# A first feed-forward group without partial products, and three small moves in the order of GpSimd, ScalarE and VectorE work

## The chip, the cores and the metric

The kernel runs on one core of one Trainium2 chip. The metric is device time in microseconds from the first to the last instruction. Before the change it is 1409.2 us, the median of three runs (1407.0 to 1409.7). The profiled execution has a span of 1406.5 us, with a mean granted TensorE clock of 0.99.

## The reference, cut to what matters

Two blocks follow each other. The first is attention with a threshold, for 8 batches, 8 heads, 576 positions and a head width of 64; the second is a layer norm with a feed-forward block and a residual, on 512 features with 2048 hidden ones.

```python
scores = scale * np.matmul(q, k.transpose(0, 1, 3, 2))
thresh = np.max(scores, axis=-1, keepdims=True) - tau
scores = np.where(scores >= thresh, scores, -1000000000.0)
scores = scores - np.max(scores, axis=-1, keepdims=True)
attn = np.exp(scores)
attn = attn / (np.sum(attn, axis=-1, keepdims=True) + 1e-09)
return np.matmul(attn, v).astype(np.float32)
...
x = np.ascontiguousarray(attn_out.transpose(0, 2, 1, 3)).reshape(B, S, H * D)
...
xn = (x - mu) / np.sqrt(var + 1e-06) * g_ln
ch = np.maximum(xn @ w_ch1, 0.0) @ w_ch2
return (x + ch).astype(np.float32)
```

All of it is in float32.

## The kernel before, in words

**Two streams, interleaved.** Attention goes in 72 *slots*, nine for each of the 8 batches (`NS = B * SLOTS`, L65). Slots s = 0 to 3 and 5 to 8 of a batch treat a pair of heads and one half of its rows; slot 4 (`HP`) treats what is left over of all pairs. In a slot TensorE makes the scores (L394), VectorE takes their maxima (L408, `exponentials`), GpSimd makes the thresholds (L412), ScalarE the exponentials (L418), VectorE applies the threshold and sums the rows (L426), inverts the sums (L431), and GpSimd divides (L442, `weights`). VectorE then transposes the result by blocks into `et` (L508), which goes to memory and comes back as `em` for the product with the values in the next slot (L554). In the first batch this transposition is done by TensorE instead (L466, L482).

**The feed-forward groups.** When half of a batch's positions have their 512 features, they make a *group* of 288 tokens; there are 16 groups, two to a batch. `centre` (L606) subtracts the mean (L613) and leaves `xc`. Then `ffn_steps` (L1003) makes a generator that yields after each product on TensorE: `first_part` (w_ch1, ReLU, into `hidden`), then the second part (w_ch2), `second_plain` for group 0 and `second_quarters` for the others. Even groups start in slot 6 of their batch, odd ones in slot 2 of the next batch; groups 0 and 1 start in slots 6 and 10 of the whole.

**Tiles and quarters.** A *tile* is 128 hidden features for all 288 tokens: 8 matmuls (four `product` calls of two matmuls of 64 columns, L104), and a ReLU on ScalarE (L805). In all groups but group 0 six of the 16 tiles (`SETS`, 5 to 7 and 13 to 15) are replaced by seven *quarters*: a fast scheme of the Strassen-Winograd kind, which makes seven half-sized products in place of eight and needs sums and differences. The differences of the activations are three GpSimd operations (`less`, `add`, `less` at L842 to L844, into `t3`, `t2`, `t4`) and one on VectorE (`t1`, L848); the results are added on VectorE and GpSimd (L755) and clipped (L761). A quarter's bank is copied by ScalarE (L838). The differences of the weights are made once: `differences_1` (L703, eight operations on GpSimd and VectorE in a chain that goes back and forth between them) for w_ch1, `differences` (L719, 16 operations) for w_ch2. In the second part of the groups from 1 on, seven *segments* of 16 `product` calls each do the same for w_ch2 (L931 to L945), with differences of `hidden` on both engines (L929). Tiles, quarters and segments share two banks of PSUM (`ps_ff`, L79), so a product waits for the copy of the last but one.

**The norm.** `norm` (L773) is called after each tile and each quarter. It first has ScalarE square `xc` (L777) into a part of `hidden` that is free until later, and GpSimd add the four squares (L779, three additions). Some steps later it puts a product of these sums with a constant matrix on TensorE (`var`, L784), ScalarE turns it into a first root (L786 to L788), and three VectorE operations improve it (`root`, L674 to L678). `ended` counts finished tiles, `part` is the part of the slot in which the call falls.

**What sets the order.** The schedule is written out by hand: each engine works through its list in the order of these Python calls. A slot has four parts. `second_part` (L1037) is called once in each; it adds to `owed` the units that this part should do, from the units left in the group and from `ROOM` (L1013), shared out over the time to the next group's start, and steps the generator until it is used up:

```python
owed += (ends[g] - issued) * ROOM[i] / left if left > 0 else 8
got = 1 if i in (0, QUARTERS - 1) else 2
while queue and (owed >= 0.5 or got == 1 and i in (0, QUARTERS - 1)):
    got, cost = next(queue[0], (None, 0))
```

So parts 0 and 3 end only at the end of a tile, quarter or segment; parts 1 and 2 end anywhere. A tile costs 4 units, a quarter 3, a variance product 1, a segment 8. Between the parts lie the attention's own calls: in order, scores, maxima, two exponentials, part 0, two more exponentials, `turn` (the transposes of the next q and k, with a product on GpSimd, L342), part 1, `weights`, `drip`, part 2, `turn_blocks`, `drip`, the product with the values, part 3, `drip`.

**Lists of later calls.** `later` (L741) puts an operation into `rush` or `drops` with an engine, a cost and an age; `drip` (L622) issues those that are urgent and ripe, or for which there is room; `need` (L750) issues them at once where a product needs them. A `rush` entry for GpSimd at the head is also issued straight after part 0 (L1108).

Of the kernel before, what the change touches and what calls it, by code (L numbers as in the profile page):

```python
# [18 lines left out]
def kernel(  # L19
# [31 lines left out]
    nc = tc.nc  # L51
# [5 lines left out]
    NK = DM // 128  # L57
    ND = DF // 128
# [4 lines left out]
    SLOTS = 2 * HP + 1  # L63
    NG = 2 * B
# [3 lines left out]
    HT, HD, HM = TOK // 2, ND // 2, NK // 2  # L68
    SETS = [(5, 6, 7)]
# [547 lines left out]

    aside, stores, drops, rush = [], [], [], []  # L620

    def drip(room=None, everything=False):  # L622


        room = dict(room or {})
        for calls in (rush, drops):
            urgent = [i for i, d in enumerate(calls) if d[0] and d[1] <= now]
            n = urgent[-1] + 1 if urgent else 0
            while calls:
                _, ripe, eng, cost, go = calls[0]  # L630
                if n <= 0 and not everything:
                    if ripe >= now or room.get(eng, 0) < cost:
                        break
                    room[eng] -= cost
                calls.pop(0)
                n -= 1
                go()
# [112 lines left out]
    def need(calls, done, *what):  # L750
        while not done.issuperset(what):
            calls.pop(0)[-1]()

    def add(eng, out, a, b):
        eng.tensor_tensor(out=out, in0=a, in1=b, op=ALU.add)  # L755

    def less(eng, out, a, b):
        eng.tensor_tensor(out=out, in0=a, in1=b, op=ALU.subtract)
# [4 lines left out]
    def first_part(g, done):  # L763
# [1 line left out]

        xc = centred.pop(g)
        plain = g == 0
        low = ND - NK if plain else ND - 3 - NK
        sq = hidden[:, low : low + NK]
        rb, squared, ended = [], [], 0  # L770
        sums_of = differences() if g == 1 else iter(())

        def norm(must=False):  # L773

            if ended and not squared and (plain or part):
                squared.append(ended)
                nc.scalar.activation(sq, xc, func=AF.Square)  # L777
                for c in range(1, NK):
                    nc.gpsimd.tensor_tensor(out=sq[:, 0], in0=sq[:, 0], in1=sq[:, c], op=ALU.add)  # L779
            elif squared and not rb and (  # L780
                ended >= squared[0] + (7 if plain else 2) and part > (0 if plain else 1) or must
            ):
                var = ps_ff.tile([128, TOK], F32, tag="ff", name="var")
                product(var, lhsT=avg_sb, rhs=sq[:, 0], start=True, stop=True)  # L784
                rb.append(ffn.tile([128, TOK], F32, tag="rb", bufs=2, name="rb"))
                nc.scalar.activation(sq[:, 2], var, func=AF.Identity, bias=eps_sb)  # L786
                nc.scalar.activation(rb[0], sq[:, 2], func=AF.Ln)
                nc.scalar.activation(rb[0], rb[0], func=AF.Exp, scale=-0.5)  # L788
                later(
                    rush, done, ("root", 3, lambda _: root(rb[0], sq[:, 2], sq[:, 3]), nc.vector),  # L790
                    urgent=nc.vector, age=2 if part > 2 else 0,
                )
                return [(1, 1)]
            return []
# [44 lines left out]
            yield 2, 0.5  # L839

        def quarters():
            less(pool, t3, b22, b12)  # L842
            add(pool, t2, b11, t3)
            less(pool, t4, b21, t2)  # L844
            yield quarter(1, old(0, 0), b11, h11)
            yield quarter(2, old(0, 1), b21)
            yield quarter(7, s3, t3)
            later(rush, done, ("xt1", 1, less, dve, t1, b12, b11), urgent=dve)  # L848
            yield quarter(6, s2, t2, h12)
            later(  # L850
                rush, done, ("xu2", 1, add, dve, h12, h12, h11), ("xu3", 1, add, dve, parts[7], parts[7], h12),
                ("x11", 1, add, pool, h11, h11, parts[2]), ("r11", 1, positive, pool, h11),
            )
            need(rush, done, "xt1")
            yield quarter(4, old(1, 1), t4, h21)
            later(rush, done, ("x21", 1, add, dve, h21, h21, parts[7]), ("r21", 1, positive, dve, h21))
            need(rush, done, "x11")
            yield quarter(3, s4, b22)
            later(rush, done, ("x12", 1, add, dve, h12, h12, parts[3]))
            yield quarter(5, old(1, 0), t1, h22)  # L860
            later(
                rush, done, ("xu4", 1, add, dve, h12, h12, h22), ("r12", 1, positive, dve, h12),
                ("x22", 1, add, dve, h22, h22, parts[7]), ("r22", 1, positive, dve, h22),
                urgent=dve,
            )

        paired = set() if plain else {m + i for m in ms for i in (0, HD)}
        singles = [d for d in range(ND) if d not in paired]
        between = iter(()) if plain else quarters()
        for d in singles:  # L870
            while conversion.ended < 4 * (d // 4 + 1):
                yield 0, 0
            if d == low:
                yield from norm(True)
            if d == low + 2:
                need(rush, done, "root")
            yield from tile_of(d)
            for _ in range(2):
                next(sums_of, None)
            ended += 1  # L880
            yield from norm()
            if not plain and d > 1:
                yield from next(between, ())
                yield from norm()
        for more_of in between:
            yield from more_of
# [3 lines left out]

    def second_plain(g, rb, done):
        y = ffn.tile([128, NK, TOK], F32, tag="sq", bufs=1, name="y")
        sums_of = differences_1()
        for m in range(NK):
            p2 = ps_ff.tile([128, TOK], F32, tag="ff", name="p2")
            for d in range(ND):
                while conversion.ended <= conversion.n1 + 4 * m + d // 4:
                    yield 0, 0
                product(
                    p2, lhsT=w2_sb[:, m, d], rhs=hidden[:, d],  # L900
                    start=(d == 0), stop=(d == ND - 1),
                )
                if now >= QUARTERS * (SLOTS + 1) and d % 2:
                    next(sums_of, None)
                if d < ND - 1:
                    yield 2, 1
            aside.append(lambda m=m, p2=p2: add_to_x(g, m, y[:, m], p2, rb))
            yield 2, 1
        for _ in sums_of:
            pass  # L910

    def second_quarters(g, rb, done):


# [2 lines left out]
        s2, s3, s4 = more  # L917
        b11, b12 = hidden[:, :HD, early], hidden[:, :HD, late]
        b21, b22 = hidden[:, HD:, early], hidden[:, HD:, late]
        need(rush, done, "r21")  # L920
        while drops:
            drops.pop(0)[-1]()
        y = ffn.tile([128, NK, TOK], F32, tag="sq", bufs=1, name="y")
# [2 lines left out]
        def by_fours(eng, out, in0, in1, op):  # L926
            for d in range(0, HD, 4):
                at = (slice(None), slice(d, d + 4))
                eng.tensor_tensor(out=out[at], in0=in0[at], in1=in1[at], op=op)  # L929

        def segment(weights, rhs, out=None):  # L931
            bank = ps_ff.tile([128, HM, HT], F32, tag="ff", name="seg")
            for d in range(HD):
                for m in range(HM):
                    at, end = (d, m), (HD - 1, HM - 1)
                    product(
                        bank[:, m], lhsT=weights[:, m, d], rhs=rhs[:, d],
                        start=at == (0, 0), stop=at == end,
                    )
                    if at != end:  # L940
                        yield 2, 0.5
            if out is None:
                out = part_tile("part")[:, : HM * HT].rearrange("p (m t) -> p m t", t=HT)
            nc.scalar.copy(out, bank)
            return out  # L945
# [49 lines left out]
        while waiting_mean:  # L995
            mean_of(waiting_mean.pop(0))
        p3 = yield from last
        later(drops, done, ("12", 1, add, dve, y12, y12, p3), ("done12", 2, finish, pool, 0, 1, (0, 1)))
        yield 2, 0.5

# [2 lines left out]
    def ffn_steps(g):  # L1003
# [7 lines left out]


    ROOM = (0.6, 1.0, 1.25, 0.35)  # L1013
    STEPS = [1 + NK * ND * 2] + [
        1 + NK * ND * 2 - NK * ND // 8 - sum(NK * len(ms) for ms in SETS) // 4
    ] * (NG - 1)
    ends = [sum(STEPS[: i + 1]) for i in range(NG)]
    queue = []
    issued = part = now = 0
# [70 lines left out]
    for n in range(NS):  # L1090
# [74 lines left out]
        tick(6)  # L1165
        run_all(aside)
        drip({nc.vector: 2, nc.gpsimd: 0})
    while later_calls or queue or aside or stores or drops or rush:
        n += 1
        for i in range(QUARTERS):  # L1170
            run(n, i)
            second_part(n, i)
            run_all(aside)
            drip(everything=True)
            run_all(stores)
# [30 lines left out]
```

## Time and profile before

| what | value |
|---|---|
| median of three runs | 1409.2 us (1407.0 to 1409.7) |
| span of the profiled execution | 1406.5 us |
| VectorE busy | 1013.2 us, 72% |
| GpSimd busy | 725.2 us, 52% |
| ScalarE busy | 497.6 us, 35% |
| matmul of 288 columns in a tile, x2656 | 410 ns each as recorded, 351.9 us together |
| matmul of 144 columns in a quarter (`hidden`), x1440 | 289 ns each as recorded, 101.9 us together |
| GpSimd division L442, x252 | 840 ns each |
| GpSimd sum of squares L779, x48 | 878 ns each |
| VectorE maximum L408, x144 | 1350 ns each |

How to read it: the busy time of TensorE is the union of its records, which overlap, so 410 ns of one matmul isn't what it adds to the time; the distance between the starts of two tiles in the timeline is. The profile writes a tile's four products as 16 matmul records, and a quarter's six products as 24. PEld is the loading of weights, which overlaps the matmuls. "Waits" lists, for an engine and a line, how long it stood and what ended that. Busy shares are means over 72 slots; what a change in one slot is worth is read in the timeline of that slot.

### The profile page before, as it was taken

How to read it: one execution, taken by the hardware profiler on the slowest of the kernel's cores; microseconds unless marked ns; L12 is line 12 of the kernel's file. 1: busy time of each engine (PE TensorE's matmuls, PEld its weight loads, DVE VectorE, ACT ScalarE, POOL GpSimd, SP SyncE). 2: the span in 40 equal slices, each digit the busy share in tenths (PEclk: the TensorE clock that was granted, in tenths of full speed). 3: DMA queues.
4: the chain of work that ended last, by engine and by line, in shares of the span. 5: the costliest groups of instructions: out<-in, count | busy, mean ns of one | idle time of the engine just before them, and what ended most of it. 6: DMA issues, size and time to landing. Idle time of an engine off the chain costs nothing. (4 is left out here: it accounts for less than half of the span.)

```text
span 1406.5 us, 38066 instructions
## 1 busy us (share of the span) xinstructions
PE 1326.8 (94%) x16128; PEld 1043.7 (74%) x16128; DVE 1013.2 (72%) x1680; ACT 497.6 (35%) x985; POOL 725.2 (52%) x887
## 2 busy tenths in 40 slices
PE   4888979899999999999999999999999999999996
PEld 3665656677868777787968777786868777787876
DVE  5997867668777787877777787877877687777321
ACT  3877613133242423333232323333242333324120
POOL 2444445655455655555554654546554644656433
PEclk9999999999999999999999999999999999999998
DMA  9612345255855376455855376445755377444211
GB/s 230 172 62 84 92 113 150 100 184 144 202 157 165 123 199 154 144 178 140 216 153 170 108 197 186 144 158 152 199 161 166 124 190 182 145 145 144 77 18 18
DMA packets 316393, 205.64 MB, mean 146 GB/s; under 512 B 242368, under 2 KB 273856, under 8 KB 308160
## 3 DMA queue, kind: packets, MB, share of 16 engines
q1 hardware_dynamic: 311456, 202.62, 50.6%
q8 instruction: 127, 2.08, 0.6%
q10 hardware_dynamic: 4736, 0.59, 0.4%
q14 instruction: 42, 0.34, 0.1%
q0 software_dynamic: 32, 0.00, 0.0%
HBM read 119.41 MB, written 83.76 MB: 144 GB/s over the span
## 5 line engine op out<-in xcount | busy, mean ns | idle before, releaser
L104 PE MATMUL p<-xc,w 128*64 128x288 f32 x2656 | 351.9, 410 | 15.2 <-DVE xc L613 9.8
L408 DVE TENSOR_REDUCE neg<-sc 128x2 f32<-128x1152 f32 x144 | 188.5, 1350 | 230.6 <-PE sc L394 230.6
L104 PEld LDWEIGHTS p<-xc,w 128*64 128x64 f32 x2656 | 190.4, 138 | 131.2 <-DVE xc L613 15.3
L418 ACT ACTIVATE e<-sc,neg 128x576 f32<-128x576 f32 x288 | 197.3, 745 | 249.3 <-DVE neg L408 217.1
L442 POOL TENSOR_SCALAR e<-e,den 128x576 f32<-128x576 f32 x252 | 208.6, 840 | 115.2 <-DVE den L431 115.0
L104 PE MATMUL seg<-hidden,w 128*64 128x144 f32 x3840 | 247.3, 286 | 1.5 <-DVE hidden L929 1.5
L104 PEld LDWEIGHTS seg<-hidden,w 128*64 128x64 f32 x3840 | 234.9, 137 | 11.9 <-issue 7.6
L426 DVE SCALAR_TENSOR_TENSOR e<-sc,thr,e 128x576 f32<-128x576 f32 x288 | 222.4, 811 | 12.8 <-ACT e L418 12.1
L412 POOL TENSOR_SCALAR thr<-neg,low_sb 128x2 f32<-128x2 f32 x144 | 44.7, 310 | 256.2 <-DVE neg L408 251.9
L508 DVE STREAM_TRANSPOSE et<-e 128x1152 f32<-128x1152 f32 x112 | 150.8, 1363 | 24.7 <-POOL e L442 24.3
L394 PE MATMUL sc<-kT,qT 64*128 64x192 f32 (+3 forms) x1024 | 149.1, 424 | 19.6 <-DVE qT L354 10.0
L394 PEld LDWEIGHTS sc<-kT,qT 64*128 64x128 f32 x1024 | 93.7, 190 | 66.9 <-issue 16.9
L554 PE MATMUL sc<-em,v_in 128*64 128x256 f32 (+1 forms) x1408 | 132.4, 331 | 2.5 <-DMA em<-scr 1.9
L104 PE MATMUL seg<-hidden,stage 128*64 128x144 f32 x1920 | 123.4, 287 | 0.0
L104 PEld LDWEIGHTS seg<-hidden,stage 128*64 128x64 f32 x1920 | 117.6, 137 | 5.4 <-issue 4.0
L805 ACT ACTIVATE hidden<-p 128x288 f32<-128x288 f32 x166 | 68.6, 414 | 148.9 <-PE p L104 148.3
L104 PE MATMUL quarter<-hidden,w 128*64 128x144 f32 x1440 | 101.9, 289 | 14.7 <-ACT part L838 14.6
L104 PEld LDWEIGHTS quarter<-hidden,w 128*64 128x64 f32 x1440 | 88.8, 137 | 34.4 <-POOL thr L412 10.7
L554 PEld LDWEIGHTS sc<-em,v_in 128*64 128x64 f32 x1408 | 87.8, 138 | 31.4 <-DMA em<-scr 2.1
L929 POOL TENSOR_TENSOR hidden<-hidden 128x576 f32<-128x576 f32 x60 | 89.0, 1492 | 42.1 <-DVE hidden L761 26.0
L104 PEld LDWEIGHTS quarter<-xc,w 128*64 128x64 f32 x1080 | 67.5, 137 | 13.0 <-ACT hidden L805 4.3
L571 ACT COPY x<-sc 128x256 f32<-128x256 f32 x60 | 22.3, 372 | 154.3 <-PE sc L554 152.6
(175 smaller groups left out, 1639.2 us busy)
## 6 DMA issues: line engine op xcount, KB each, us to landing
scr<-et SPq DMA_DIRECT2D x63, 1152.0 KB, 4.4
em<-scr SPq DMA_DIRECT2D x63, 1024.0 KB, 5.9
out_dram<-x SPq DMA_DIRECT2D x256, 36.0 KB, 4.3
q_in<-in_q_dram SPq DMA_DIRECT2D x124, 72.0 KB, 3.5
k_in<-in_k_dram SPq DMA_DIRECT2D x120, 72.0 KB, 2.8
er<-scr SPq DMA_DIRECT2D x63, 128.0 KB, 5.9
v_in<-in_v_dram SPq DMA_DIRECT2D x28, 256.0 KB, 4.4
w<-in_moe_w_ch_dram SPq DMA_DIRECT2D x10, 512.0 KB, 5.5
```

What stands on the lines that cost most here:

```text
L104: nc.tensor.matmul(out[r], lhsT=lhsT[:, r], rhs=rhs, **flags)
L394: nc.tensor.matmul(sc[h][64 * i : 64 * i + 64 if s == HP else 128, at : at + n], lhsT=ql[r] if s == HP else qT[r, half, j * 128 : (j + 1) ...
L408: nc.vector.tensor_reduce(out=neg[:, i], in_=pairs[h], axis=AXL.X, op=ALU.max, negate=True,)
L412: nc.gpsimd.tensor_scalar(out=thr[:, i], in0=neg[:, i], scalar1=-1.0, scalar2=low_sb, op0=ALU.mult, op1=ALU.add,)
L418: nc.scalar.activation(es[:, i], blocks[i], func=AF.Exp, bias=neg[:, i : i + 1])
L426: nc.vector.scalar_tensor_tensor(out=es[:, i], in0=blocks[i], scalar=thr[:, i : i + 1], in1=es[:, i], op0=ALU.is_ge, op1=ALU.mult, accum_o ...
L442: nc.gpsimd.tensor_scalar(out=es[:, i], in0=es[:, i], scalar1=den[:, i : i + 1], scalar2=1.0, op0=ALU.mult, op1=ALU.mult,)
L508: nc.vector.transpose(et[:, :, 64 * h : 64 * h + 64].rearrange("p n (j c) -> p j n c", j=2), es[:, 2 * h : 2 * h + 2].rearrange("p j (n c) ...
L554: nc.tensor.matmul(dst[64 * h : 64 * h + 64], lhsT=vt[:, h, c, :] if c < J else vr[:, h, :], rhs=pick(em[:, :, c] if c < J else er, hp, h) ...
L571: nc.scalar.copy(x_of(g)[:, hp, :QH], pv)
L805: nc.scalar.activation(hidden[:, d], p1, func=AF.Relu)
L929: eng.tensor_tensor(out=out[at], in0=in0[at], in1=in1[at], op=op)
```

## The change

It has five parts.

1. **Group 1 plain in its first part.** `whole` (groups 0 and 1) takes the place of `plain` where the tiles are chosen: group 1 makes 16 tiles and no quarters. Its second part stays as it is. The differences of w_ch2, made during group 1's first part, go one to a tile instead of two. `STEPS` counts group 1's units accordingly (121 instead of 118).
2. **Differences of w_ch1 later.** As group 1 no longer needs them, they move from group 0's second part, in slot 10, to the segments of group 1's second part, two to a segment.
3. **Early differences in a third list.** The three GpSimd operations ahead of the quarters no longer stand in the generator's order; they go into a list `early_on`, which `drip` empties first, or `need` before quarter 7.
4. **Squares in the slot's second half.** For all groups but group 0 the squares wait for part 2 or 3 (`part > 1`), and quarters count in `ended`.
5. **Root later.** The root step always gets an age of two parts, where it had none if the variance product fell in parts 0 to 2.

Parts 3 to 5 are meant to let the attention's divisions and maxima go ahead of the norm's work.

```diff
-        for calls in (rush, drops):
+        for calls in (early_on, rush, drops):
...
         plain = g == 0
-        low = ND - NK if plain else ND - 3 - NK
+        whole = g < 2
+        low = ND - NK if whole else ND - 3 - NK
...
-            if ended and not squared and (plain or part):
+            if ended and not squared and (plain or part > 1 or must):
...
-                    urgent=nc.vector, age=2 if part > 2 else 0,
+                    urgent=nc.vector, age=2,
...
         def quarters():
-            less(pool, t3, b22, b12)
-            add(pool, t2, b11, t3)
-            less(pool, t4, b21, t2)
+            later(
+                early_on, done, ("xt3", 1, less, pool, t3, b22, b12),
+                ("xt2", 1, add, pool, t2, b11, t3), ("xt4", 1, less, pool, t4, b21, t2), urgent=pool,
+            )
             yield quarter(1, old(0, 0), b11, h11)
             yield quarter(2, old(0, 1), b21)
+            need(early_on, done, "xt4")
             yield quarter(7, s3, t3)
...
-        paired = set() if plain else {m + i for m in ms for i in (0, HD)}
+        paired = set() if whole else {m + i for m in ms for i in (0, HD)}
...
             if d == low:
                 yield from norm(True)
+                yield from norm(True)
...
             yield from tile_of(d)
-            for _ in range(2):
-                next(sums_of, None)
+            next(sums_of, None)
             ended += 1
             yield from norm()
-            if not plain and d > 1:
+            if not whole and d > 1:
                 yield from next(between, ())
+                ended += 1
                 yield from norm()
...
     def second_plain(g, rb, done):
-        sums_of = differences_1()
...
-                if now >= QUARTERS * (SLOTS + 1) and d % 2:
-                    next(sums_of, None)
...
     def second_quarters(g, rb, done):
...
+        sums_of = differences_1() if g == 1 else iter(())
...
+                if d % 4 == 3:
+                    next(sums_of, None)
...
-    STEPS = [1 + NK * ND * 2] + [
-        1 + NK * ND * 2 - NK * ND // 8 - sum(NK * len(ms) for ms in SETS) // 4
-    ] * (NG - 1)
+    STEPS = [
+        1 + NK * ND * 2 - (NK * ND // 8 if g else 0) - (NK * len(SETS[0]) // 4 if g > 1 else 0)
+        for g in range(NG)
+    ]
```

More of the change, by code (lines that the diff above doesn't have):

```diff
@@ L615, in centre @@
             )
-    aside, stores, drops, rush = [], [], [], []
+    aside, stores, drops, rush, early_on = [], [], [], [], []
     def drip(room=None, everything=False):
         room = dict(room or {})
-        for calls in (rush, drops):
+        for calls in (early_on, rush, drops):
             urgent = [i for i, d in enumerate(calls) if d[0] and d[1] <= now]
@@ L865, in quarters @@
             )
-        paired = set() if plain else {m + i for m in ms for i in (0, HD)}
+        paired = set() if whole else {m + i for m in ms for i in (0, HD)}
         singles = [d for d in range(ND) if d not in paired]
-        between = iter(()) if plain else quarters()
+        between = iter(()) if whole else quarters()
         for d in singles:
@@ L908, in second_plain @@
             yield 2, 1
-        for _ in sums_of:
-            pass
     def second_quarters(g, rb, done):
@@ L919, in second_quarters @@
         b21, b22 = hidden[:, HD:, early], hidden[:, HD:, late]
-        need(rush, done, "r21")
+        if g > 1:
+            need(rush, done, "r21")
         while drops:
@@ L997, in second_quarters @@
         p3 = yield from last
+        for _ in sums_of:
+            pass
         later(drops, done, ("12", 1, add, dve, y12, y12, p3), ("done12", 2, finish, pool, 0, 1, (0, 1)))
@@ L1167 @@
         drip({nc.vector: 2, nc.gpsimd: 0})
-    while later_calls or queue or aside or stores or drops or rush:
+    while later_calls or queue or aside or stores or drops or rush or early_on:
         n += 1
```

## The prediction

> **What bounds the kernel now.** I read the page's busy times first, then the waits of TensorE alone, then timelines of the stretches in which TensorE has gaps.
>
> ```profile
> PE 1326.8 (94%) x16128; PEld 1043.7 (74%) x16128; DVE 1013.2 (72%) x1680; ACT 497.6 (35%) x985; POOL 725.2 (52%) x887
> ```
>
> TensorE is busy for 1326.8 of 1406.5 us and runs its list in order, so what counts is what lengthens or fills its 80 us of idle time. TensorE's waits in total, times, longest:
>
> ```profile
> PE quarter L104 <- ACT part L838: 14.6, 13, 4.8
> ...
> PE p L104 <- DVE xc L613: 9.8, 3, 7.8
> ...
> PE var L104 <- POOL hidden L779: 1.2, 6, 0.2
> ```
>
> They lie in few places. From 300 us to 1300 us one gap of about 1.3 us comes back in each batch, in the slot after an odd group starts. Timeline around it (start, length, engine, operation, [idle before]): TensorE, then GpSimd, then VectorE.
>
> ```profile
> 553.09 2.11 PE L104 MATMUL p<-xc,w 128*64 128x288 f32 x16
> 555.40 0.71 PE L104 MATMUL var<-hidden,avg_sb 128*64 128x288 f32 x4 [0.20 <-POOL hidden L779]
> 555.93 1.64 PE L104 MATMUL quarter<-xc,w 128*64 128x144 f32 x24
> 557.40 1.90 PE L554 MATMUL sc<-em,v_in 128*64 128x256 f32 x16
> ...
> 568.68 1.69 PE L104 MATMUL quarter<-hidden,w 128*64 128x144 f32 x24 [1.31 <-ACT part L838]
> ```
>
> ```profile
> 552.70 2.64 POOL L779 TENSOR_TENSOR hidden<-hidden 128x288 f32<-128x288 f32 x3 [3.06 <-ACT hidden L777]
> 555.30 1.02 POOL L758 TENSOR_TENSOR hidden<-xc 128x288 f32<-128x288 f32 x1
> 556.40 0.90 POOL L755 TENSOR_TENSOR hidden<-xc,hidden 128x288 f32<-128x288 f32 x1
> 557.38 0.81 POOL L758 TENSOR_TENSOR hidden<-xc,hidden 128x288 f32<-128x288 f32 x1
> 558.17 2.91 POOL L442 TENSOR_SCALAR e<-e,den 128x576 f32<-128x576 f32 x4
> ```
>
> ```profile
> 552.05 0.17 DVE L431 RECIPROCAL den<-den 128x2 f32<-128x2 f32 x1
> ...
> 562.86 1.55 DVE L677 TENSOR_TENSOR hidden<-hidden 128x288 f32<-128x288 f32 x1
> 564.45 0.95 DVE L678 SCALAR_TENSOR_TENSOR rb<-hidden,rb 128x288 f32<-128x288 f32 x1
> 565.32 2.61 DVE L408 TENSOR_REDUCE neg<-sc 128x2 f32<-128x1152 f32 x2
> ```
>
> The denominators are there at 552.2, but GpSimd divides (L442) only at 558.2, behind the sums of squares (L779) and the early differences (L758, L755). Then the transposes and the root run late, the maximum (L408) starts 1.5 us after the scores end, the exponentials follow, and the copy of a quarter's bank stands behind them: 1.3 us for TensorE. The variance product waits for the sums of squares by 0.20 us only: they are just in time.
>
> The other place is group 1. In slot 10 VectorE stands twice before differences of w_ch1, and the centring comes late:
>
> ```profile
> 204.10 0.56 DVE L712 TENSOR_TENSOR w<-w,w 128x384 f32<-128x384 f32 x1 [2.06 <-POOL w L710]
> ...
> 208.86 3.05 DVE L613 TENSOR_TENSOR xc<-x,sum 128x288 f32<-128x288 f32 x4
> ```
>
> TensorE idles there from 202.00 to 209.79. In its quarters it loses 0.59 us (232.9), 1.13 us (244.6) and 4.80 us (254.9, a bank whose copy waits for GpSimd), and at 291.1 it waits 1.87 us for a tile's transfer.
>
> **The Trainium skill.** "Perfetto Trace Analysis", Tensor Engine Instruction, says that ScalarE, VectorE and GpSimd are strict FIFO; the trace agrees, since L442 waits 6 us for nothing but its place. "SBUF — State Buffer", Who interferes with whom: a VectorE instruction with two SBUF inputs contends with a GpSimd one that reads SBUF. It agrees: L677 takes 1.55 us beside GpSimd at 562.9 and 0.46 us alone at 238.9. "GPSIMD Engine Reference", Engine selection: two-input operations are about half as fast there; L758 with 128x288 is 884 ns on GpSimd, 426 ns on VectorE.
>
> **The change, part by part.**
>
> *Differences of w_ch1.* Eight operations leave slot 10. Without them VectorE's list there is: maximum to 197.3, four transposes of q and k (1.7 us) behind q_in of GpSimd (to about 199.4), one store transpose 0.4, four threshold products with reciprocals 3.33 (205.17 to 208.50), one product 0.44. The centring starts at 203.55 instead of 208.86: 5.3 us less on TensorE's path. In group 1's second part they go two to a segment of 4 us; GpSimd (1.0 us each) and VectorE (0.56) have idle time there, since group 1 has no quarters' sums left; nothing on the path.
>
> *Group 1 plain.* Six tiles take the place of seven quarters. By starts in the timeline a tile takes 2.1 us and a quarter 1.47 to 1.5: 12.6 - 10.4 = +2.2 us of TensorE. The stalls that came with the quarters' additions go: -0.6, -1.1, -4.8. In slot 13 VectorE no longer has five additions of quarters (267.0 to 271.0) ahead of its threshold products, so the weights leave 4 us earlier, and the wait of 1.9 us for the transfer goes too. w_ch2's differences go one to a tile instead of two: the same 16 operations, spread out. Front in sum: -5.3 - 6.5 - 1.9 + 2.2 = -11.5 us, ends -9 and -14.
>
> *Odd groups 3 to 13 (six times).* I work out by the pacing rule what falls into which part of slot 2 of a batch. A group has 118 units for 14.4 of room: parts 0 to 3 get 4.9, 8.2, 10.2 and 2.9. Part 0 ends with tile 1, overdrawn by 2.8. Part 1 has 5.4: tile 2 (4 units) and two of quarter 1's six products; the early differences are queued there. Part 2 starts with 10.6; quarter 1's other products take 2 and leave about 8.4. In the kernel before, the squares came at the head of part 1, and part 2 went tile (4), variance (1), quarter 2 (3), as the trace has it. After, squares need part 2: they come behind quarter 1's copy. Quarters now count in "ended", so it is 4 there; tile 3 and quarter 2 make it 6, two more, with 1.4 units left of the 0.5 needed: the variance product (1 unit) is issued in the same part, straight behind quarter 2.
>
> GpSimd's list becomes: divisions, early differences (drip behind the weights), sums of squares. Divisions: the first two from 552.3, 1.47 us; the others from 554.0 (second reciprocal at 553.72), between 1.46 us alone and 2.4 us beside VectorE's additions (as at 572.08): to 555.4 or 556.4. Differences 3 x 0.88 = 2.65, sums 3 x 0.88 = 2.64: ready at 560.7 to 561.7. TensorE, without the variance in between: the tile ends at 555.20, quarter 2 takes 1.47, so it wants the sums at 556.67. It stands 4.0 to 5.0 us; I take 4.6. Behind the variance product in its list stand the value products (L554), tile 4 and the next slot's scores, and behind these VectorE's maximum and all of that slot; nothing takes up the delay. Against it: the old 0.2 goes, and the 1.3 us stall nearly all, since VectorE is free when the scores come, and the root now runs behind the next slot's threshold products, which no TensorE instruction waits for before tile 11: -1.2. Each time 4.6 - 0.2 - 1.2 = +3.2 us (2.5 to 3.6); six times +19.2 (15 to 21.6).
>
> *Last group.* No attention beside it, so no divisions. Squares come after tile 3 (its ReLU ended at 1346.7), 1.2 + 2.6 us later the sums are there, 1350.5; TensorE wants them after quarter 2 and tile 4, at 1349.5: +1.0.
>
> *Even groups, group 0.* Squares fell in part 2 and the variance in part 3 already; the third list lets the differences go at the end of the same part, with nothing of GpSimd between. The later root of group 0 lies in VectorE's idle time of slot 7. 0. Step counts move with the work: 0.
>
> Sum: -11.5 + 19.2 + 1.0 = +8.7; 1409.2 + 8.7 = 1418.
>
> **Rivals.** (B) The variance product isn't in TensorE's way: it comes behind other work, or GpSimd is done in time. For it: in the even groups the squares go well in the second half. Against it: GpSimd has 8.2 us of work between 552.3 and the variance, and 4.4 us of time. Then -11.5 - 6 x 1.3 + 1 = -18: 1391. (D) It is issued one part later, behind the value products (2.2 us): the stall is 2.3, each group +0.9; -11.5 + 5.4 + 1 = -5: 1404. Against it: 1.4 units left, three times what is needed. (C) The front gives half, because the moved differences put VectorE behind GpSimd in slots 13 and 14 as they did in slot 10 (1.4 + 2.1 us there), or the transfer's wait stays: +5.8, 1424. For it: the same pairs, same chain; against it: idle time of 10 us on VectorE at 264.
>
> **How the numbers follow.** My forecast 0.64, B 0.12, C 0.12, D 0.12. Low ends of my terms, -14 + 15 + 0.5, give 1411, high ends, -9 + 21.6 + 1.5, 1423. The range from 1403 to 1425 takes in D and C and leaves B and a few per cent out. Faster: B, nearly all of D and a trace of mine, 0.23; within 0.2%: 0.06; slower 0.71.
>
> **What would show it.** Right: the wait of the variance product for L779 grows from 1.2 us in six to over 24 us in six; L442 starts near 552 in that slot, L779 near 558; the 1.3 us gaps of the quarters go; centring in slot 10 starts near 203.5, and TensorE's gap at 202 is 2.5 us; slot 15 begins about 11 us earlier. Wrong: no wait of the variance product in the odd groups, or its place behind L554; or new gaps in slots 11 to 15.

## The result, and the profile after

The changed kernel takes 1422.5 us (median of four runs, 1421.6 to 1424.1) against 1408.2 us of the kernel before, measured beside it: ratio 1.0102, with a 95% interval from 1.0085 to 1.0120. The forecast was 1418, slower, in a range from 1403 to 1425.

The profiled span grew by 13.4 us, from 1406.5 to 1419.9. TensorE's busy time and its waits, from the page and the waits of TensorE of the kernel after:

```profile
PE 1333.4 (94%) x16056; PEld 1037.7 (73%) x16056; DVE 996.4 (70%) x1670; ACT 497.6 (35%) x984; POOL 718.6 (51%) x882
```

```profile
PE var L104 <- POOL hidden L780: 27.8, 7, 4.8
...
PE p L104 <- DVE xc L613: 4.5, 4, 2.2
...
PE quarter L104 <- ACT part L839: 2.0, 6, 0.3
```

The waits for the centring and for the quarters' banks went down (9.8 to 4.5 us, 14.6 to 2.0 us). The wait of the variance product for GpSimd's sums of squares went up from 1.2 to 27.8 us. VectorE and GpSimd have less to do than before and ScalarE as much, and the kernel is slower.

The timelines of slot 29, the same stretch of group 5 as was shown of before, TensorE and then GpSimd:

```profile
542.59 2.11 PE L104 MATMUL p<-xc,w 128*64 128x288 f32 x16
544.53 1.64 PE L104 MATMUL quarter<-xc,w 128*64 128x144 f32 x24
550.62 1.01 PE L104 MATMUL var<-hidden,avg_sb 128*64 128x288 f32 x4 [4.45 <-POOL hidden L780]
551.41 3.33 PE L554 MATMUL sc<-em,v_in 128*64 128x256 f32 x16
```

```profile
541.83 1.47 POOL L442 TENSOR_SCALAR e<-e,den 128x576 f32<-128x576 f32 x2 [2.69 <-DVE den L431]
543.48 2.08 POOL L442 TENSOR_SCALAR e<-e,den 128x576 f32<-128x576 f32 x2 [0.18 <-DVE den L431]
545.53 0.80 POOL L758 TENSOR_TENSOR hidden<-xc 128x288 f32<-128x288 f32 x1
...
548.04 2.53 POOL L780 TENSOR_TENSOR hidden<-hidden 128x288 f32<-128x288 f32 x3
```

GpSimd now divides as soon as the denominators are there, as the change intends. The early differences and then the sums of squares stand behind that, and the sums are ready at 550.6. TensorE is through with its second quarter by 546.2 and stands for 4.45 us. Look also at the line below the wait: the 16 records of the value products take 3.33 us, where the same 16 took 1.90 us before. A window of the profile shows what goes with it. Its columns are the stretch and its length, busy times and counts of TensorE, weight loads, VectorE, ScalarE and GpSimd, then the granted clock (the share of TensorE's full clock that the chip let through), the DMA share and GB/s:

```profile
552.00:554.00 2.00, 2.00 (x14) 1.08 (x12) 0.00 (x0) 1.14 (x3) 1.99 (x2) 0.50 0.00 0
```

The granted clock is 0.50 behind the wait. The trace records a stretch at half the clock at each of the six waits: of 3.41 us at four of them, and of 6.83 us at two (groups 3 and 11).

In slot 10 the centring and TensorE's first products on it, VectorE and then TensorE:

```profile
201.98 3.05 DVE L613 TENSOR_TENSOR xc<-x,sum 128x288 f32<-128x288 f32 x4
```

```profile
202.91 1.91 PE L104 MATMUL p<-xc,w 128*64 128x288 f32 x12 [2.20 <-DVE xc L613]
```

TensorE waits there for 2.2 us, and then 0.27 us for the next piece of `xc`, where it waited 7.79 us.

To see where the time goes, I measure by the starts of the maxima (L408): "front" is from slot 10 to slot 15, a "batch" from slot 28 to slot 37, which holds one even and one odd group of the steady state. What lies ahead of slot 10 varies by some 3 us over these profiles (193.4 to 196.7 us), with stretches of half the clock near the start, and is left out.

| kernel | front, us | a batch, us | wait of the variance product | median, us |
|---|---|---|---|---|
| before | 102.5 | 160.0 | 0.2 | 1408.2 to 1409.2 |
| after | 87.9 | 164.3 | 4.45 | 1422.5 |
| front_only | 87.9 | 159.8 | 0.2 | 1393.4 |
| order_only | 108.6 | 164.2 | 4.42 | 1442.7 |
| no_third_list | 87.9 | 160.0 | 1.94 | 1398.9 |
| sums_first | 87.9 | 160.1 | 1.94 | 1398.9 |
| squares_early | 87.9 | 158.5 | 0.24 | 1386.3 |
| var_later | 87.9 | 158.6 | none | 1388.4 |
| root_early | 87.9 | 164.2 | 4.4 | 1421.1 |
| keep_warm | 87.9 | 164.7 | none, behind 6.8 of filling | 1425.1 |
| keep_warm8 | 88.8 | 162.5 | 0.57, behind 3.9 of filling | 1412.1 |
| plain_only | 92.9 | 159.8 | 0.2 | 1399.5 |
| squares_early_seg | 92.4 | 158.5 | 0.2 | 1390.7 |

The front became 14.6 us shorter. From slot 15 to the end the kernel after is 29.3 us longer: five batches from slot 19 to slot 64 take 823.4 instead of 799.2 us, and the rest, with the sixth odd group and the last one, 5.2 us more. With 1.3 us less ahead of slot 10 that is the 13.4 us. The front of keep_warm8 is 0.9 us longer than the others', with a wait of 0.66 us for a transfer in slot 14, where no filling is.

### The profile page after: what moved, and what is told of

The parts are those of the page before. It is cut to its first block, busy times and chain, and to the rows that moved or that the text cites. A ratio compares the mean times of both kernels' runs of the same rounds, so it can differ in the third digit from the quotient of the medians.

```text
span 1419.9 us, 37871 instructions
## 1 busy us (share of the span) xinstructions
PE 1333.4 (94%) x16056; PEld 1037.7 (73%) x16056; DVE 996.4 (70%) x1670; ACT 497.6 (35%) x984; POOL 718.6 (51%) x882
## 5 line engine op out<-in xcount | busy, mean ns | idle before, releaser
L408 DVE TENSOR_REDUCE neg<-sc 128x2 f32<-128x1152 f32 x144 | 188.7, 1352 | 279.6 <-PE sc L394 279.5
L104 PE MATMUL p<-xc,w 128*64 128x288 f32 x2752 | 361.8, 409 | 8.8 <-DVE xc L613 4.5
L104 PEld LDWEIGHTS seg<-hidden,w 128*64 128x64 f32 x3840 | 235.0, 137 | 11.7 <-issue 7.2
L554 PE MATMUL sc<-em,v_in 128*64 128x256 f32 (+1 forms) x1408 | 139.2, 343 | 0.0
L928 POOL TENSOR_TENSOR hidden<-hidden 128x576 f32<-128x576 f32 x60 | 89.4, 1500 | 40.0 <-DVE hidden L761 24.0
L104 PEld LDWEIGHTS quarter<-hidden,w 128*64 128x64 f32 x1344 | 82.3, 137 | 19.6 <-ACT part L839 7.0
L104 PE MATMUL quarter<-hidden,w 128*64 128x144 f32 x1344 | 94.4, 288 | 2.1 <-ACT part L839 2.0
L104 PEld LDWEIGHTS quarter<-xc,w 128*64 128x64 f32 x1008 | 62.5, 137 | 12.5 <-ACT hidden L806 3.7
```

The source lines that it names most:

```text
L104: nc.tensor.matmul(out[r], lhsT=lhsT[:, r], rhs=rhs, **flags)
L408: nc.vector.tensor_reduce(out=neg[:, i], in_=pairs[h], axis=AXL.X, op=ALU.max, negate=True,)
L554: nc.tensor.matmul(dst[64 * h : 64 * h + 64], lhsT=vt[:, h, c, :] if c < J else vr[:, h, :], rhs=pick(em[:, :, c] if c < J else er, hp, h) ...
```

## The experiments

My theory was the sum of the prediction: the front gains, each odd group loses more, because the variance product stands too early in TensorE's list for the sums that GpSimd now makes last. The rivals were another cause in the odd groups (the late squares by themselves, the later root), and, since the value products were seen to slow down, an effect of idle time on the clock or none.

**The two halves apart.** front_only is the kernel after with parts 3 to 5 of the change undone, order_only the kernel before with these parts alone.

```diff
# front_only, against after
-            later(early_on, done, ("xt3", ...), ("xt2", ...), ("xt4", ...), urgent=pool)
+            less(pool, t3, b22, b12)
+            add(pool, t2, b11, t3)
+            less(pool, t4, b21, t2)
...
-            need(early_on, done, "xt4")
...
-            if ended and not squared and (plain or part > 1 or must):
+            if ended and not squared and (plain or part or must):
-                ended += 1          # the one behind a quarter
-                    urgent=nc.vector, age=2,
+                    urgent=nc.vector, age=2 if part > 2 else 0,
```

> The kernel after with its parts 3 to 5 undone: group 1 plain and the differences of w_ch1 in its second part, the order of squares, early differences and root as before. My theory (two effects of opposite sign: the front gains some 15 us, the odd groups lose some 29): slot 15 begins 15 to 16 us earlier than before, the odd groups have their old gaps (variance 0.2 us, quarter 1.3 us), the time is 1393 (1390 to 1396). Rival (the front isn't worth more than the 11.5 us that I forecast, and the rest of the loss lies elsewhere): 1397 to 1400.

It takes 1393.4 us, ratio 0.9896 (0.9879 to 0.9912), with batches as before. So the first two parts alone are a gain of 15 us.

> The kernel before with parts 3 to 5 alone: early differences in the third list, squares in the second half, root later; group 1 keeps its quarters and the differences of w_ch1 stay in slot 10. My theory: six waits of the variance product of 4.4 us, each followed by a stretch at half the granted clock, the 1.3 us gaps gone; 1437 (1433 to 1441). Rival (idle time alone, no clock): 6 x 3 = +18, 1427.

It takes 1442.7 us, ratio 1.0243 (1.0228 to 1.0258). The six waits are there, 4.42 us each. The time is more than I expected, by a cost that group 1 alone has: with its quarters kept, quarter 7 comes in the same slot as the third list, and waits 5.88 us for the early differences behind the divisions; the front is 6.1 us longer than before. In the steady state quarter 7 comes a slot later and doesn't wait. So in group 1 the third list has a price of its own, which part 1 of the change takes away.

**What in the odd groups makes the wait.** Three kernels change one thing each in the kernel after.

```diff
# no_third_list: the early differences at once, as before; squares in the second half
-            later(early_on, done, ("xt3", ...), ("xt2", ...), ("xt4", ...), urgent=pool)
+            less(pool, t3, b22, b12)
+            add(pool, t2, b11, t3)
+            less(pool, t4, b21, t2)
...
-            need(early_on, done, "xt4")
# sums_first: the third list, but behind the sums of squares
-                ..., urgent=pool,
+                ..., urgent=pool, age=1 if g % 2 else 0,
# squares_early: part 4 undone, the third list and the later root kept
-            if ended and not squared and (plain or part > 1 or must):
+            if ended and not squared and (plain or part or must):
-                ended += 1          # the one behind a quarter
```

> The kernel after with part 3 undone: the three early differences are issued at once, in part 1, as before; squares stay in the second half. My theory (what counts is when GpSimd has the sums of squares; it stands idle for 2.7 us before the first reciprocal, and the differences, 2.6 us, fit in there): the variance product waits 1.7 to 2.0 us instead of 4.4, the clock does not drop, the quarter gaps stay away; 6 x (2.6 + 2) = 28 less than after, 1394. Rival A (the squares in the second half make the whole wait, wherever the differences stand): 1421 to 1424. Rival B (no cost of the clock): 6 x 2.6 less, 1407.

> The kernel after with one number changed: the early differences of odd groups get an age of one part, so that GpSimd has them behind the sums of squares and not ahead. Same work, same lists. My theory (the place of the sums in GpSimd's list makes the wait): the variance product waits 4.45 - 2.6 = 1.9 us, the clock drops seldom; 1397 to 1401, as without the third list. Rival (it is the lateness of the squares on ScalarE): 1422.

> The kernel after with part 4 undone: squares from part 1 on, quarters not counted; the third list and the later root stay. My theory: the sums are ready as before (wait of the variance product 0.2 us), the divisions start at about 2.7 us later than in the kernel after but 2.8 us earlier than before, so the maxima are on time and the 1.3 us gaps stay away; 1386 (1384 to 1390). Rival (divisions behind the sums are late enough to bring the quarter gaps back): 1393.

no_third_list: 1398.9 us, 0.9937 (0.9922 to 0.9951). Its GpSimd list in that slot:

```profile
538.76 0.80 POOL L758 TENSOR_TENSOR hidden<-xc 128x288 f32<-128x288 f32 x1
...
541.49 1.46 POOL L442 TENSOR_SCALAR e<-e,den 128x576 f32<-128x576 f32 x2 [0.16 <-DVE den L431]
...
545.18 2.53 POOL L780 TENSOR_TENSOR hidden<-hidden 128x288 f32<-128x288 f32 x3
```

And the variance product on TensorE:

```profile
547.77 0.71 PE L104 MATMUL var<-hidden,avg_sb 128*64 128x288 f32 x4 [1.94 <-POOL hidden L780]
```

The differences fill the 2.7 us in which GpSimd waited for the first reciprocal; the divisions begin on time all the same, and the sums are ready 2.5 us sooner. sums_first, with the same operations in another order, has the same wait (1.94 us) and the same time: 1398.9 us, 0.9926 (0.9910 to 0.9943). In both kernels the squares are as late as in the kernel after, so the late squares alone don't make the whole wait: 2.5 of the 4.45 us are the differences, which stood between the divisions and the sums. The other 1.94 us stay, because part 4 of the change still puts the squares, and with them the sums, behind the divisions. Rival A of no_third_list falls, and rival B, 1407, as well: the gain is 23.6 us, where six times 2.5 us of wait are 15. A batch is 4.3 us shorter: 2.5 us of wait and 1.8 us more. My own 1394 was too low by 5 us, mostly because I had expected no drop of the clock, and there are two, at the first and the sixth wait.

squares_early: 1386.3 us, 0.9845 (0.9830 to 0.9860), the lowest median of all (var_later, below, can't be told from it). Its GpSimd list:

```profile
537.83 2.64 POOL L780 TENSOR_TENSOR hidden<-hidden 128x288 f32<-128x288 f32 x3 [3.11 <-ACT hidden L778]
540.46 3.38 POOL L442 TENSOR_SCALAR e<-e,den 128x576 f32<-128x576 f32 x4
543.82 0.80 POOL L758 TENSOR_TENSOR hidden<-xc 128x288 f32<-128x288 f32 x1
```

The sums come first and the variance product waits 0.24 us; the divisions are ahead of the differences and so early enough that the old quarter gap of 1.3 us goes, but for 0.28 us in one batch. The kernel has the gain of the front and of the earlier divisions, and not the wait. So the third list alone makes no wait, the late squares alone make one of 1.94 us, and both together 4.45 us.

**The variance product later, the root earlier.** The other way to take the wait away is to leave GpSimd's order and move the product:

```diff
# var_later
-                ended >= squared[0] + (7 if plain else 2) and ...
+                ended >= squared[0] + (7 if plain else 4 if g % 2 else 2) and ...
# root_early: part 5 undone
-                    urgent=nc.vector, age=2,
+                    urgent=nc.vector, age=2 if part > 2 else 0,
```

> The kernel after with the variance product of odd groups asked for four finished steps behind the squares in place of two: it then falls in the next slot, ahead of tile 9. Squares, list and root as after. My theory (only a product that comes too early in TensorE's list waits): no wait of the variance product, no quarter gaps; 1386 (1384 to 1390). Rival (the root comes too late and tile 11 waits for it): a new wait of 1 to 2 us each, 1392 to 1398.

> The kernel after with part 5 undone: the root of odd groups runs at the end of part 2 of its slot. My theory: TensorE stands until the variance product, so VectorE has 12 us of idle time there, and the root fits in wherever it is; no change, 1422 (1420 to 1425). Rival (it is the root that brought the 1.3 us gaps): 1430.

var_later takes 1388.4 us, 0.9852 (0.9838 to 0.9867): squares, sums and third list are as late as in the kernel after, the product stands ahead of tile 9 in the next slot, and nothing waits:

```profile
553.64 0.69 PE L104 MATMUL var<-hidden,avg_sb 128*64 128x288 f32 x4
```

The rival's wait of tile 11 for the root is not there. This and squares_early show the cause from both sides: it is the distance between the sums in GpSimd's list and the product in TensorE's. root_early takes 1421.1 us, 1.0083 (1.0068 to 1.0098), not to be told from the kernel after: beside the other parts, part 5 of the change costs nothing and brings nothing.

**What a wait costs beside its length.** To part the idle time from the clock, I fill the wait with products whose result is overwritten. They leave nothing out; they add work.

```diff
# keep_warm (14 products), keep_warm8 (8 products)
+                if g % 2 and 1 < g < NG - 1:
+                    for _ in range(14):
+                        product(var, lhsT=avg_sb, rhs=xc[:, 0], start=True, stop=True)
                 product(var, lhsT=avg_sb, rhs=sq[:, 0], start=True, stop=True)
```

> The kernel after with 14 products more on TensorE in each odd group from 3 to 13, straight ahead of the variance product and into its own bank, which that product then overwrites: 3.7 us of work (14 x 0.265) that depends on nothing, in place of idle time. The variance product can start no sooner and no later. Theory with the clock: TensorE stands 0.7 us in place of 4.45, the granted clock does not drop, and the time is shorter although more work is done: 6 x 1.4 to 1.7, and two longer drops, about 10 to 12 us less than after, 1411. Rival without the clock: 1422, no change.

It takes 1425.1 us, 1.0114 (1.0098 to 1.0129). I had mis-sized the filling: a product takes 0.485 us and not 0.265, so 14 took 6.8 us and outlasted the wait. The clock stayed up, though, and a batch takes 164.7 us, hardly more than the 164.3 us of the kernel after, though the filling outlasts the wait by more than 2 us. So once more with 8:

> As the kernel with 14 products in place of idle time, but with 8: the run before showed 0.485 us for such a product (14 took 6.8 us), not 0.265, so that 14 outlasted the wait by 2.2 us. Eight take 3.9 us and fit into the wait of 4.45. Theory with the clock: the variance product starts when it did, no drop of the clock behind it, the value products take 2.2 us in place of 3.6; 1.7 us less in each of six groups and 1.2 more in the two with the longer drop: 11 to 13 us less than after, 1410. Rival without the clock: 1422.

It takes 1412.1 us, 1.0020 (1.0010 to 1.0030): some 10 us less than the kernel after, with 48 products more. TensorE's timeline and a window of it:

```profile
547.12 4.05 PE L104 MATMUL var<-xc,avg_sb 128*64 128x288 f32 x32
551.74 0.71 PE L104 MATMUL var<-hidden,avg_sb 128*64 128x288 f32 x4 [0.57 <-POOL hidden L780]
552.28 1.90 PE L554 MATMUL sc<-em,v_in 128*64 128x256 f32 x16
```

```profile
552.00:556.00 4.00, 4.00 (x38) 2.55 (x36) 0.00 (x0) 1.76 (x4) 3.84 (x4) 1.00 0.20 53
```

From the start of quarter 2 to the variance product it is 6.09 us in both kernels, 545.65 to 551.74 here and 544.53 to 550.62 in the kernel after. So the variance product is held up as long; only the clock differs, 1.00 in place of 0.50, and the value products take 1.90 us again. Batch by batch, keep_warm8 takes 1.4 to 1.8 us less than the kernel after where that has a drop of 3.41 us, and 2.3 and 2.9 us less where it has one of 6.83 us. Over five batches these are 813.4 in place of 823.4 us.

**The parts of the front.** plain_only makes group 1 plain and nothing else; the differences of w_ch1 stay in slot 10. They change a block of w_ch1 in place, so that group 1's tiles 13 to 15 are made with changed weights in this kernel; the instructions stay the same.

> The kernel before with group 1 plain in its first part, and nothing else: the differences of w_ch1 stay in slot 10, order of squares, early differences and root as before. My theory: TensorE waits 7.5 us for the centring in place of 2.2, and then has half the clock for some us; 5.3 + 3 us more than with both front parts, 1401 to 1402, slot 13 has no wait of its segment for GpSimd. Rival (the quarters alone were what cost in the front, the place of the differences doesn't matter): 1393.

It takes 1399.5 us, 0.9934 (0.9919 to 0.9949). TensorE waits 7.23 us for the centring, and half the clock goes with it for 6.83 us; the front is 5.1 us longer than front_only's. So the place of the differences is worth 5 us net, and the rival falls, though I had expected more (8 us). It would be more if the move had no price:

```profile
252.39 1.01 POOL L710 TENSOR_TENSOR w<-w 128x384 f32<-128x384 f32 x1
253.38 3.51 POOL L442 TENSOR_SCALAR e<-e,den 128x576 f32<-128x576 f32 x4
256.86 2.76 POOL L928 TENSOR_TENSOR hidden<-hidden 128x576 f32<-128x576 f32 x2
```

```profile
258.31 0.47 PE L104 MATMUL seg<-hidden,stage 128*64 128x144 f32 x4 [1.54 <-POOL hidden L928]
```

These are GpSimd and TensorE of the kernel after in slot 13: one difference of w_ch1 (L710) is ahead of the divisions and of the differences of `hidden` (L928), for which the third segment waits 1.54 us. In plain_only that wait isn't there. I tried to take it away in squares_early, by starting with these differences two segments later:

```diff
# squares_early_seg, against squares_early
-                if d % 4 == 3:
+                if d % 4 == 3 and len(begun) > 2:      # begun: one entry for each segment
```

> The fastest kernel so far (after with part 4 undone), with the differences of w_ch1 from the third segment of group 1 on in place of the first. My theory: the wait of 1.5 us in slot 13 for GpSimd's differences of hidden goes, since these stand behind one difference of w_ch1 less; 1.0 to 1.5 us less, 1385 (1383 to 1387), which can hardly be told from the noise, but the wait can. Rival (divisions and w_ch2 differences make that wait): it stays at 1.5 us.

The wait in slot 13 is gone, but the time is 1390.7 us, 0.9868 (0.9852 to 0.9885), 4 us more than without. VectorE in slot 14:

```profile
277.25 1.13 DVE L712 TENSOR_TENSOR w<-w,w 128x384 f32<-128x384 f32 x1 [3.50 <-POOL w L710]
278.30 2.01 DVE L927 TENSOR_TENSOR hidden<-hidden 128x576 f32<-128x576 f32 x2
```

A difference of w_ch1 on VectorE waits 3.5 us for its partner on GpSimd, which stands behind the divisions; behind it waits a difference of `hidden`, and for that TensorE, 4.4 us, with a drop of the clock of 3.41 us. It is the same chain between two engines that cost in slot 10 of the kernel before.

## Why the prediction was right, point by point, and which terms were off

- **The wait of the variance product**: forecast 4.0 to 5.0 us, taken 4.6; measured 4.45 (4.79 in group 3). The pacing put it where I had worked it out, straight behind quarter 2 and ahead of the value products, and GpSimd's list has the order that I wrote down; rivals B and D, which needed the product elsewhere, fell.
- **What goes against it**: the quarter gap of 1.3 us and the old 0.2 us. Both go. The waits of 0.33 us that the page still shows for a quarter lie in other slots, and front_only, which has the old gaps of 1.3 us, has them too.
- **The sum of an odd group was mis-sized**: "Each time 4.6 - 0.2 - 1.2 = +3.2 us". With the measured terms it is 4.45 - 0.2 - 1.3 = 2.95 us, and keep_warm8, where the clock stays up, shows 2.8 us in the mean of five batches (813.4 against 799.2). With the drops it is 4.8 us (823.4). The term that was missing is the half clock that goes with a wait of this length, 2.0 us in the mean. From slot 15 to the end I forecast 20.2 us with the last group; keep_warm8 has 17.6 us there, and the kernel after 29.3. It could have been read: the Trainium skill, "TensorE: Matmul & The Clock Gate", What's actually happening, says that TensorE falls to half its clock when it has been idle for about 3.4 us and needs about 3.4 us of work to come back; and in the trace of before 16 records of value products take 3.19 us right behind its gap of 4.80 us, at a clock of 0.50:

```profile
254.92 0.75 PE L104 MATMUL quarter<-hidden,w 128*64 128x144 f32 x4 [4.80 <-ACT part L838]
255.46 3.19 PE L554 MATMUL sc<-em,v_in 128*64 128x256 f32 x16
```

- **The front was mis-sized the other way**: forecast -11.5, measured -14.6 us. The centring's 5.3 us came as worked out (7.79 to 2.20 and 0.27), and so did the gaps of the quarters and of the transfer. Three terms were off. "Nothing on the path" for the moved differences failed: they cost 1.54 us in slot 13, where rival C had named a cost, though here it is GpSimd that comes late and not VectorE. "By starts in the timeline a tile takes 2.1 us" is a wrong reading: 2.11 us is the length of a tile's records, and from start to start it is 1.94 us (542.59 to 544.53 above; the median of before is the same), so six tiles in place of seven quarters cost +1.2 and not +2.2 us. With these two the terms give -11.0. The third is again the clock: in the kernel before, 10.24 us at half the clock go with the two long gaps, and TensorE works in 7.03 us of them, which at half speed costs about 3.5 us by estimate; in the kernel after, the front has none. Then the sum is -14.5. The clock's part in it is worked out and not shown by a run of its own.
- **Last group**: forecast +1.0, measured 0.77 us.
- **Even groups, group 0 and the root**: forecast 0; root_early shows no difference for the root. The even groups and group 0 have no run of their own.

So the mechanism was right on both sides, and each long wait costs more than its length, which I had put at nothing. This term stands on both sides of the sum: some 3.5 us in the front, once, and 11.7 us behind it. That the time came out only 4.5 us above the forecast is in part luck: had the front gained no more than I forecast, the odd groups' loss would have brought it to 1425.6 us, past the upper end of my range.

## What to carry to other kernels

When an operation of a helper engine is put off, look at what its reader has in its own list by then: moving the producer back and the consumer forward, as here, turns a wait of 0.2 us into one of 4.4. Before putting work in order of urgency, see whether the engine is idle ahead of the urgent work: three differences in 2.7 us of idle time did not hold up the divisions, and behind the divisions they cost 2.5 us. And count a wait of TensorE of some microseconds with the slower clock that goes with it; work that depends on nothing, put in its place, was worth 10 us here, and taking the wait away was worth 34 to 36 us.

## What the runs showed of the hardware that I had not expected

- With each of the 18 waits of 4.4 to 4.8 us of the variance product (after, order_only, root_early) TensorE was granted half its clock, for 3.41 us in 14 of them and for 6.83 us in four.
- A shorter wait can do it too. In no_third_list and sums_first the first wait, 2.28 and 2.29 us, had a drop of 3.41 us both times, and so had one of the ten waits of 1.93 to 1.95 us that followed; the wait of 2.2 us for the centring in slot 10 of the kernel after had none. The traces show what sets them apart. In each of the 13, the clock changes only in steps: the times between its changes are whole multiples of 3.413 us, so that they lie on a grid. What counts is how much of a wait falls into one step of the grid. The sixth wait of no_third_list lies in one step whole (first line: TensorE is busy for 1.47 of 3.41 us), and the next step has half the clock. The second wait, as long, is split into 0.88 and 1.05 us, and the clock stays up (here and in the step after, third and fourth line):

```profile
1185.01:1188.42 3.41, 1.47 (x24) 1.20 (x22) 2.59 (x3) 0.78 (x2) 3.25 (x5) 1.00 0.00 0
1188.42:1191.83 3.41, 3.41 (x18) 1.90 (x16) 0.00 (x0) 1.39 (x3) 3.27 (x3) 0.50 0.83 346
...
546.72:550.13 3.41, 2.36 (x22) 1.59 (x24) 0.43 (x1) 1.39 (x3) 3.25 (x4) 1.00 0.74 277
550.13:553.54 3.41, 3.41 (x30) 1.98 (x28) 0.00 (x0) 0.78 (x2) 2.69 (x4) 1.00 0.51 109
```

- From 150 us of each trace to the half clock with which it ends, all 28 drops of the 13 traces follow a step with at least 1.94 us of idle time of TensorE, and of the steps at full clock with that much only one, with 2.02 us (the wait in slot 10 of the kernel after), had no drop behind it. Half the clock lasted for a second step where TensorE was idle for 0.80 us or more of the first, as in group 11 of the kernel after (0.94 us), and ended where it was idle for 0.66 us or less. A wait of 4.4 us has at least 2.2 us in one step however it falls, which fits that it always cost the clock. The page of the Trainium skill named above gives about 3.4 us of idle time for the drop; here about 2 us in one step was enough, and the measurement decides.
